# Dense TensorE products in the waits of the first units, and two bonus products on VectorE

## The chip, the cores and the metric

The kernel runs on one core of a Trainium2 chip. The metric is the device time of one execution in microseconds (us); three runs of the kernel before are given, and one execution was profiled. [...]

## The reference, cut to what matters

An RWKV-like attention with a state per head, then a soft mixture of experts, then a feed-forward layer with a squared ReLU. The change touches the attention alone:

```python
B, H, S, D = r.shape                      # 4, 8, 768, 48
for t in range(S):
    kt, vt, rt = (k[:, :, t], v[:, :, t], r[:, :, t])
    cur = np.einsum('bhd,bhe->bhde', u[None] * kt, vt)
    y[:, :, t] = np.einsum('bhd,bhde->bhe', rt, state + cur)
    state = w[None, :, :, None] * state + np.einsum('bhd,bhe->bhde', kt, vt)
```

The part with `u` is the bonus: token t sees its own key and value with the weight sum over d of r * u * k.

## The kernel before, in words

The attention is cut into 16 units (NU): a batch and a pair of heads each, n = 0 to 15. A unit has six chunks of 128 tokens (NC), taken in two groups g of three (GC). Each unit has r, k transposed (`tr`, loaded by L92 in two halves) and k, r, v with tokens on the partitions (`krv`, loaded by L96 in two halves) in one of four buffers (NB), so the loads of unit n + 4 are issued when unit n has let go of its buffer.

The steps of a unit are small functions, and the order of the instructions on each engine is the order in which they are called (the schedule is written out by hand; each engine runs its own queue in order):

- `decay(n, m)`, L232: VectorE multiplies the transposed r (m = 0) or k (m = 1) by a table of powers of w, which lies in PSUM (`tab`).
- `bonus(n)`, L237 and L238: GpSimd multiplies r by u, then by k, both in place. Each product is 128x576.
- `weigh(n)`, L242: VectorE sums that over d into `dg`, the diagonal's values.
- `keys(n)`, L248: GpSimd (VectorE for unit 0) multiplies k by powers of w (`pkn`).
- `diag(n, g)`, L254: GpSimd spreads `dg` onto the diagonal of `AT` by an affine select. AT has three buffers.
- `A(n, g)`, L264: TensorE makes the scores of three chunks and two heads, in two PSUM banks; `strict(n, g)`, L270: VectorE copies the part above the diagonal into `AT` and so frees the two banks.
- `KV(n)`, L278: TensorE makes the sums over a chunk of k times v; `scan(n)`, L283: VectorE scans them over the chunks, and ScalarE copies the result to `SB` (L285).
- `Y(n, g)`, L301 and L307: TensorE multiplies by the state and by AT; ScalarE copies out (L313).
- `X(n, g)`, L320, and `L(n)`, L335: TensorE turns the outputs and makes the logits of the experts, one unit later.
- `keep_clock(k)`, L225: k fp32 products of the identity with itself, 128x128 by 128x256, into a bank of the tag "tr" that nobody reads. The trace shows each as two instructions.

Ahead of the loop stand the tables: the powers of w on VectorE (L193 to L208), their transposes on TensorE (L424), the copy to `pkn` (L425), and the first steps of unit 0 (L417 to L438). In the loop, iteration n calls A(n, 1); keys, weigh, diag(., 0) and decay(., 1) of unit n + 1; strict(n, 1); X(n - 1, 0); Y(n, 0); KV(n + 1) and diag(n + 1, 1); L(n - 1); A(n + 1, 0), scan and strict(n + 1, 0); X(n - 1, 1); Y(n, 1); bonus(n + 2) and decay(n + 2, 0); and then the loads of unit n + 4 and mostly one load of an expert's weights (1536 KB).

After the attention come the experts (L540 to L582) and the feed-forward layer (L725 to L817), whose weights are loaded as buffers come free.

Of the kernel before, what the change touches and what calls it, by code (L numbers as in the profile page):

```python
# [24 lines left out]
ALU = mybir.AluOpType  # L25
# [4 lines left out]
def rwkv_softmoe_ffn(ctx: ExitStack, tc: tile.TileContext, tr, krv, wt, u, phi, w1, w2, w_in, w_out, out):  # L30
    nc = tc.nc
    NU, _, _, S = tr.shape
    D = phi.shape[0] // (2 * wt.shape[1])
    NROW, NHALF = 12 * (S // 128) * D // 2, krv.shape[-1] // 2
    NP = wt.shape[1]
    H = 2 * NP
    B = NU // NP
    NC = S // 128
# [21 lines left out]
    def ps(tag):  # L60
        cnt[0] += 1
        return psum.tile([128, 512], F32, name=f"ps_{tag}{cnt[0]}", tag=tag, bufs=BANKS[tag])

    def wk(shape, tag, bufs, dt=F32, pool=None):
        cnt[0] += 1
        return (pool or work).tile(shape, dt, name=f"{tag}_{cnt[0]}", tag=tag, bufs=bufs)
# [14 lines left out]
    def t_view(n):  # L81

        return units[n % NB][:112, :2 * S].rearrange("p (m c t) -> p m c t", m=2, c=NC)

    def n_view(n):

        return units[n % NB][:, 2 * S:].rearrange("p (m c h d) -> p m c h d", m=3, c=NC, h=2)
# [13 lines left out]
    U = att.tile([128, NP, 2, D], F32, name="U")  # L101
# [95 lines left out]
    for i in range(6):  # L197
        n = 1 << i
# [21 lines left out]
    def keep_clock(n):  # L220

        if n:
            p = ps("tr")
        for _ in range(n):
            nc.tensor.matmul(p[:, :256], ident, ident.unsqueeze(1).to_broadcast([128, 2, 128]), start=True, stop=True)  # L225


    def decay(n, m):

        x = t_view(n)[:, m]  # L230
        t = tab[:, n % NP] if m else tab[:, n % NP, ::-1]
        nc.vector.tensor_tensor(x, x, t.unsqueeze(1).to_broadcast([112, NC, 128]), ALU.mult)  # L232

    def bonus(n):

        kv_, rv = n_view(n)[:, 0], n_view(n)[:, 1]
        nc.gpsimd.tensor_tensor(rv, rv, U[:, n % NP].unsqueeze(1).to_broadcast([128, NC, 2, D]), ALU.mult)  # L237
        nc.gpsimd.tensor_tensor(rv, rv, kv_, ALU.mult)  # L238

    def weigh(n):  # L240
        dg = wk([128, NC, 2], "dg", 2)
        nc.vector.reduce_sum(dg, n_view(n)[:, 1], axis=AX.X)  # L242
        st[n, "dg"] = dg
# [6 lines left out]
    def diag(n, g):  # L250
        at = wk([128, GC, 2, 128], "AT", 3, pool=att)
        st[n, "AT", g] = at
        dg = st[n, "dg"][:, GC * g:GC * (g + 1)]
        nc.gpsimd.affine_select(out=at.rearrange("p c h t -> p (c h) t"),  # L254
                                in_=dg.rearrange("p c h -> p (c h)").unsqueeze(2).to_broadcast([128, 2 * GC, 128]),
                                pattern=[[0, 2 * GC], [1, 128]], compare_op=ALU.is_equal, fill=0.0, base=0, channel_multiplier=-1)

    def A(n, g):
        tv = t_view(n)
        p = [ps("A")[:, :GC * 128].rearrange("p (c t) -> p c t", c=GC) for _ in range(2)]  # L260
        for i in range(GC):
            for h in range(2):
                rows = slice(64 * h, 64 * h + D)
                nc.tensor.matmul(p[h][:, i], tv[rows, 1, GC * g + i], tv[rows, 0, GC * g + i], start=True, stop=True)  # L264
        st[n, "A", g] = p

    def strict(n, g):
        at, p = st[n, "AT", g], st.pop((n, "A", g))
        for h in range(2):
            nc.vector.copy_predicated(at[:, :, h], mask.unsqueeze(1).to_broadcast([128, GC, 128]), p[h])  # L270

    def KV(n):

        kv_, vv = n_view(n)[:, 0], n_view(n)[:, 2]
        pv = kvp[:, :D * NC].rearrange("p (d c) -> p d c", c=NC)
        for c in range(NC - 1):
            for h in range(2):
                nc.tensor.matmul(pv[64 * h:64 * h + D, :, c + 1], kv_[:, c, h], vv[:, c, h], start=True, stop=True)  # L278
# [8 lines left out]
    def Y(n, g):  # L287
        vv, tv = n_view(n)[:, 2], t_view(n)
        at, s = st.pop((n, "AT", g)), SB[n % 2]

        p = [y.rearrange("p (c t) -> p c t", t=128) for y in yp]
        chunks = range(GC * g, GC * (g + 1))
        at_of = lambda c, j: p[c % 2][64 * j:64 * j + D, (c - chunks[c % 2 != chunks[0] % 2]) // 2]
        opened = set()
        for c in chunks:
            for h in range(2 if c > 0 else 0):
                rows, j = slice(64 * h, 64 * h + D), (h + c) % 2  # L300
                nc.tensor.matmul(at_of(c, j), s[rows, c], tv[rows, 0, c],  # L301
                                 start=(c % 2, j) not in opened, stop=True, skip_group_check=True)
                opened.add((c % 2, j))
        for c in chunks:
            for j in range(2):
                h = (j + c) % 2
                nc.tensor.matmul(at_of(c, j), vv[:, c, h], at[:, c - GC * g, h],  # L307
                                 start=False, stop=True, skip_group_check=True)
        if g == 0:
            st[n, "xT"] = wk([112, NC, 128], "xT", 2, pool=att)  # L310
        for k in range(2):
            c0 = chunks[k]
            nc.scalar.copy(st[n, "xT"][:, c0:GC * (g + 1):2], p[c0 % 2][:112, :len(chunks[k::2])])  # L313
# [34 lines left out]
    def soft_exp(b):  # L348

        eT = wk([96, 2, 256], "eT", 1)  # L350
        st["eT", b] = eT
        nc.scalar.activation(eT[:, 0], st["lg", b][:96, :256], AF.Exp, bias=st["nm", b])
        nc.scalar.copy(eT[:, 1], st["lg", b][:96, :256])
        if 0 < b < B - 1:
            new = st["new", b]
            fa, fb = wk([96, 1], "fa", 2), wk([96, 1], "fb", 2)
            nc.scalar.activation(fa, nmx[:, 0:1], AF.Exp, bias=new, scale=-1.0)
            nc.scalar.activation(fb, st["nm", b], AF.Exp, bias=new, scale=-1.0)
            nc.scalar.copy(nmx[:, 0:1], new)
            st["f", b] = fa, fb  # L360
# [53 lines left out]
    nc.gpsimd.affine_select(out=maskf, in_=maskf, pattern=[[1, 128]], compare_op=ALU.is_gt, fill=0.0,  # L414
                            base=0, channel_multiplier=-1)
    nc.gpsimd.tensor_copy(mask, maskf)
    bonus(0)  # L417
    decay(0, 1)
    decay(0, 0)
    keep_clock(6)  # L420

    pp = ps("lg")
    for a in range(NP):
        nc.tensor.transpose(pp[:, a * 128:a * 128 + 112], tabs[:, a], ident[:112, :112])  # L424
    nc.scalar.copy(pkn, pp.rearrange("p (a b d) -> p a b d", a=NP, b=2)[:, :, :, :D])  # L425
    A(0, 0)
    weigh(0)
    diag(0, 0)
    keys(0, nc.vector)
    nc.scalar.copy(carry[:, :, :, 1:], pw[:, 0, :NP].unsqueeze(2).unsqueeze(3).to_broadcast([112, NP, D, NC - 1]))  # L430
    KV(0)
    strict(0, 0)
    scan(0)
    diag(0, 1)
    for i in range(2):
        nc.gpsimd.memset(xn[i][:, :, DM:DM + 1], 1.0)
    bonus(1)
    decay(1, 0)  # L438
    nload = 0
    for n in range(NU):  # L440
        nxt = n + 1 < NU
        if n == 2:

            sel = const.tile([128, 4, NS], F32, name="sel")
            nc.vector.reduce_sum(sel, ident.rearrange("p (q s) -> p s q", q=4).unsqueeze(1).to_broadcast([128, 4, NS, 4]), axis=AX.X)
            rm = const.tile([128, E], F32, name="rm")
            nc.vector.reduce_sum(rm, ident.rearrange("p (q e j) -> p e q j", q=4, e=E), axis=AX.XY)
            ones = const.tile([1, 4], F32, name="ones")
            nc.gpsimd.memset(ones, 1.0)

        b, j = divmod(n, NP)
        b -= 1
        A(n, 1)
        if nxt:
            keys(n + 1)
            weigh(n + 1)
            diag(n + 1, 0)
            decay(n + 1, 1)
        strict(n, 1)
        if n > 0:  # L460
            X(n - 1, 0)
        if b >= 0 and j == 1:
            soft_exp(b)
        Y(n, 0)
        if b >= 0 and j == 2:
            soft_sum(b)
            slots_exp(b)
        if nxt:
            KV(n + 1)
            diag(n + 1, 1)  # L470
        if n > 0:
            L(n - 1)

        if nxt:
            A(n + 1, 0)
            scan(n + 1)
            strict(n + 1, 0)
        if n > 0:
            X(n - 1, 1)
        if not nxt:  # L480
            L(n, (0,))
            X(n, 0)
        Y(n, 1)
        if b >= 0 and j == 1:
            soft_turn(b)
        if n + 2 < NU:
            bonus(n + 2)
            decay(n + 2, 0)
        if b >= 0 and j == 0:
            soft_max(b)  # L490
        if b >= 0 and j == 2:
            slots_norm(b)
        if n + NB < NU:
            load_t(n + NB)
            load_n(n + NB)
            if n not in (1, 4, 7):
                load_weight(nload)
                nload += 1
        elif n == NU - 2:
            load_win(0)  # L500
        else:
            load_weight(nload)
            nload += 1
# [382 lines left out]
```

## Time and profile before

| what | value |
|---|---|
| median of three runs | 400.87 us (400.12 to 401.17) |
| the profiled execution's own time | 400.18 us |
| its span, first to last instruction | 398.5 us |
| mean granted clock | 0.973 |
| TensorE busy | 381.7 us, 96% of the span |
| VectorE busy | 280.2 us, 70% |
| ScalarE busy | 211.7 us, 53% |
| GpSimd busy | 114.8 us, 29% |
| share of TensorE in the chain that ended last | 80% |

Shares of busy time are means over stages that differ: GpSimd works almost only in the first third of the span, and there it is busy nearly all the time. A busy TensorE is not TensorE at its peak, since matmuls are pipelined and their ends are modelled; so starts of instructions say more than their lengths.

### The profile page before, as it was taken

How to read it: one execution, taken by the hardware profiler on the slowest of the kernel's cores; microseconds unless marked ns; L12 is line 12 of the kernel's file. 1: busy time of each engine (PE TensorE's matmuls, PEld its weight loads, DVE VectorE, ACT ScalarE, POOL GpSimd, SP SyncE). 2: the span in 40 equal slices, each digit the busy share in tenths (PEclk: the TensorE clock that was granted, in tenths of full speed). 3: DMA queues.
4: the chain of work that ended last, by engine and by line, in shares of the span. 5: the costliest groups of instructions: out<-in, count | busy, mean ns of one | idle time of the engine just before them, and what ended most of it. 6: DMA issues, size and time to landing. Idle time of an engine off the chain costs nothing.

```text
span 398.5 us, 8194 instructions
## 1 busy us (share of the span) xinstructions
PE 381.7 (96%) x3219; PEld 294.2 (74%) x3219; DVE 280.2 (70%) x495; ACT 211.7 (53%) x465; POOL 114.8 (29%) x110
## 2 busy tenths in 40 slices
PE   5799999999999999789999999999999999999995
PEld 3677777767766564668787888888888888888884
DVE  5769897879974564799998567666566676566563
ACT  2224453453444451678888876555554564554552
POOL 3869997986870001122323120000000000000000
PEclk8559999999999999999999999999999999999999
DMA  7999999999995899913333202100000040000004
GB/s 245 344 320 343 389 407 403 404 404 406 405 383 188 307 410 405 375 47 102 85 100 87 63 0 104 56 0 2 0 0 2 0 159 2 0 0 2 0 0 158
DMA packets 25989, 70.81 MB, mean 178 GB/s; under 512 B 3680, under 2 KB 6112, under 8 KB 25952
## 3 DMA queue, kind: packets, MB, share of 16 engines
q1 hardware_dynamic: 25808, 70.10, 47.2%
q10 hardware_dynamic: 144, 0.20, 0.5%
q8 instruction: 25, 0.41, 0.4%
q14 instruction: 12, 0.10, 0.1%
HBM read 64.78 MB, written 4.72 MB: 174 GB/s over the span
## 4 chain that ended last, share of the span: by engine, by line
PE 80%; DMA 9%; DVE 6%; POOL 2%; issue 1%; ACT 1%; SPq 0%; POOLq 0%; ACTq 0%; DVEq 0%
PE ps_Y L817 16%; PE ps_A L817 16%; PE ps_kv L817 8%; PE ps_lg L817 8%; PE ps_A L264 7%; DMA wo<-in_w_out_dram 7%; PE ps_Y L307 5%; PE ps_Y L301 3%; PE ps_tr L320 3%; PE ps_tr L725 3%; PE ps_tab L725 3%; PE ps_lg L335 2%; DMA slot<-in_krv_dram 2%; PE ps_kv L278 2%; PE ps_tr L378 1%
## 5 line engine op out<-in xcount | busy, mean ns | idle before, releaser
L817 PE MATMUL ps_Y<-slot,slot 128*128 128x512 f32 x288 | 111.7, 395 | 0.0
L750 DVE TENSOR_TENSOR slot<-gg,slot 128x512 fp32r<-128x512 f32 (+1 forms) x97 | 66.5, 685 | 49.2 <-ACT slot L747 48.3
L817 PE MATMUL ps_A<-slot,slot 128*128 128x512 f32 x288 | 88.9, 393 | 0.6 <-DVE slot L682 0.6
L747 ACT CAST slot<-gg 128x512 fp32r<-128x512 f32 (+1 forms) x97 | 59.8, 618 | 50.5 <-DVE gg L744 49.9
L817 PEld LDWEIGHTS ps_A<-slot,slot 128*128 128x128 f32 x288 | 54.0, 188 | 13.2 <-DVE slot L682 1.0
L817 PEld LDWEIGHTS ps_Y<-slot,slot 128*128 128x128 f32 x288 | 54.1, 188 | 12.6 <-issue 0.6
L744 DVE TENSOR_TENSOR gg<-hr 128x512 f32<-128x512 f32 (+1 forms) x71 | 49.0, 691 | 14.3 <-ACT hr L737 14.2
L817 PE MATMUL ps_kv<-slot,slot 128*128 128x512 f32 x144 | 55.7, 394 | 0.0
L817 PE MATMUL ps_lg<-slot,slot 128*128 128x512 f32 x144 | 55.4, 391 | 0.0
L623 POOL TENSOR_TENSOR slot<-wf,slot 128x384 fp32r<-128x384 f32 x16 | 19.1, 1196 | 97.5 <-ACT slot L618 97.5
L270 DVE COPY_PREDICATED AT<-mask,ps_A 128x384 f32<-128x384 int32 x64 | 33.8, 583 | 9.2 <-PE ps_A L264 8.4
L264 PE MATMUL ps_A<-slot 48*128 48x128 f32 x384 | 36.2, 310 | 2.9 <-DVE slot L232 1.8
L264 PEld LDWEIGHTS ps_A<-slot 48*128 48x128 f32 x384 | 28.7, 204 | 10.3 <-DVE AT L270 3.6
L737 ACT ACTIVATE hr<-ps_tab 128x512 f32<-128x512 f32 x48 | 28.7, 599 | 12.9 <-PE ps_tab L725 12.9
L737 ACT ACTIVATE hr<-ps_tr 128x512 f32<-128x512 f32 (+1 forms) x49 | 28.8, 590 | 12.4 <-PE ps_tr L725 12.4
L313 ACT COPY xT<-ps_Y 112x256 f32<-112x256 f32 x64 | 17.4, 324 | 28.0 <-PE ps_Y L307 27.8
L254 POOL TENSOR_SCALAR_AFFINE_SELECT AT<-dg 128x768 f32<-128x768 f32 x32 | 28.0, 886 | 13.2 <-PE ps_Y L307 8.4
L817 PEld LDWEIGHTS ps_kv<-slot,slot 128*128 128x128 f32 x144 | 27.1, 188 | 6.2
L817 PEld LDWEIGHTS ps_lg<-slot,slot 128*128 128x128 f32 x144 | 27.0, 188 | 5.9
L232 DVE TENSOR_TENSOR slot<-slot,ps_tab 112x768 f32<-112x768 f32 x32 | 30.1, 941 | 0.6 <-DMA slot<-in_tr_dram 0.6
L307 PE MATMUL ps_Y<-AT,slot 128*48 128x128 f32 x384 | 29.6, 293 | 0.0
L307 PEld LDWEIGHTS ps_Y<-AT,slot 128*48 128x48 f32 x384 | 20.8, 129 | 6.5 <-issue 5.9
(168 smaller groups left out, 502.3 us busy)
## 6 DMA issues: line engine op xcount, KB each, us to landing
slot<-in_w_dram SPq DMA_DIRECT2D x14, 1536.0 KB, 11.1
slot<-in_tr_dram SPq DMA_DIRECT2D x32, 384.0 KB, 7.5
slot<-in_krv_dram SPq DMA_DIRECT2D x16, 448.0 KB, 7.3
slot<-in_krv_dram SPq DMA_DIRECT2D x16, 416.0 KB, 7.8
slot<-in_w_in_dram SPq DMA_DIRECT2D x4, 1536.0 KB, 19.1
wo<-in_w_out_dram SPq DMA_DIRECT2D x16, 384.0 KB, 3.3
out_dram<-os SPq DMA_DIRECT2D x15, 256.0 KB, 2.2
post<-in_w_dram SPq DMA_DIRECT2D x2, 1536.0 KB, 9.2
```

What stands on the lines that cost most here:

```text
L232: nc.vector.tensor_tensor(x, x, t.unsqueeze(1).to_broadcast([112, NC, 128]), ALU.mult)
L254: nc.gpsimd.affine_select(out=at.rearrange("p c h t -> p (c h) t"), in_=dg.rearrange("p c h -> p (c h)").unsqueeze(2).to_broadcast([128, 2 ...
L264: nc.tensor.matmul(p[h][:, i], tv[rows, 1, GC * g + i], tv[rows, 0, GC * g + i], start=True, stop=True)
L270: nc.vector.copy_predicated(at[:, :, h], mask.unsqueeze(1).to_broadcast([128, GC, 128]), p[h])
L307: nc.tensor.matmul(at_of(c, j), vv[:, c, h], at[:, c - GC * g, h], start=False, stop=True, skip_group_check=True)
L623: nc.gpsimd.tensor_tensor(wout_half(wls, f, WL), st.pop(("wf", f)), hi, ALU.subtract)
L725: nc.tensor.matmul(p, gst[:, 128 * f:128 * (f + 1)], cTall[:, 512 * g:512 * (g + 1)], start=True, stop=True)
L737: nc.scalar.activation(fs[i, "hr"][:, c], fs[i, "p"][:, c], AF.Relu)
L744: nc.vector.tensor_mul(gg, hr, hr)
L747: nc.scalar.copy(part(i, "gh")[:, c], fs[i, "gg"][:, c])
L750: nc.vector.tensor_tensor(part(i, "gl")[:, c], fs[i, "gg"][:, c], fs[i, "gh"].bitcast(F32)[:, c], ALU.subtract)
L817: nc.tensor.matmul(o, (hi, lo, hi)[k][:, 128 * j:128 * (j + 1)], (gh, gh, gl)[k], start=(f == 0 and k == 0), stop=(f == NF - 1 and k == 2))
```

## The change

The first product of the bonus can be put on another engine, and for units 0 and 1 that is VectorE; the second stays on GpSimd. The call of bonus(1) and that of diag(0, 1) move ahead of strict(0, 0) and scan(0). keep_clock is called with 13 in place of 6 ahead of the transposes of the table, and is called anew: 3 behind these transposes, 1 behind A(0, 0), 1 ahead of Y(0, 0) and 3 behind it (in the loop, for n = 0 alone).

```diff
-    def bonus(n):
+    def bonus(n, eng=nc.gpsimd):
 
         kv_, rv = n_view(n)[:, 0], n_view(n)[:, 1]
-        nc.gpsimd.tensor_tensor(rv, rv, U[:, n % NP].unsqueeze(1).to_broadcast([128, NC, 2, D]), ALU.mult)
+        eng.tensor_tensor(rv, rv, U[:, n % NP].unsqueeze(1).to_broadcast([128, NC, 2, D]), ALU.mult)
         nc.gpsimd.tensor_tensor(rv, rv, kv_, ALU.mult)
...
-    bonus(0)
+    bonus(0, nc.vector)
     decay(0, 1)
     decay(0, 0)
-    keep_clock(6)
+    keep_clock(13)
 
     pp = ps("lg")
     for a in range(NP):
         nc.tensor.transpose(pp[:, a * 128:a * 128 + 112], tabs[:, a], ident[:112, :112])
     nc.scalar.copy(pkn, pp.rearrange("p (a b d) -> p a b d", a=NP, b=2)[:, :, :, :D])
+    keep_clock(3)
     A(0, 0)
+    keep_clock(1)
     weigh(0)
     diag(0, 0)
     keys(0, nc.vector)
...
     KV(0)
+    diag(0, 1)
+    bonus(1, nc.vector)
     strict(0, 0)
     scan(0)
-    diag(0, 1)
     for i in range(2):
         nc.gpsimd.memset(xn[i][:, :, DM:DM + 1], 1.0)
-    bonus(1)
     decay(1, 0)
...
+        if n == 0:
+            keep_clock(1)
         Y(n, 0)
+        if n == 0:
+            keep_clock(3)
```

## Rows read from the trace of the kernel before

**Rows 1.** The page, slices: TensorE's granted clock in tenths, 40 equal slices.
```profile
PEclk8559999999999999999999999999999999999999
```

**Rows 2.** Busy by stretch: us, PE, PEld, DVE, ACT, POOL busy, PEclk, DMA share, GB/s.
```profile
28.00:29.00 1.00, 1.00 (x29) 0.94 (x28) 0.00 (x0) 0.40 (x2) 0.42 (x1) 0.81 0.83 312
...
173.20:176.60 3.40, 2.25 (x29) 1.39 (x28) 3.37 (x6) 2.94 (x6) 1.57 (x1) 1.00 0.38 118
```

**Rows 3.** Timeline of TensorE, start: start us, length us, instruction, [idle before <-releaser].
```profile
1.43 2.93 PE L225 MATMUL ps_tr<-ident 128*128 128x256 f32 x6 [1.43 <-POOL ident masks.py:199]
...
4.76 1.03 PE L225 MATMUL ps_tr<-ident 128*128 128x256 f32 x4
...
8.57 1.01 PE L424 MATMUL ps_lg<-ident,xT 112*128 112x112 f32 x4 [2.79 <-ACT xT L210]
```

**Rows 4.** The chain that ended last, 18 to 36 us: start us, us, what.
```profile
18.86 1.04 PE ps_kv L278 x20
...
27.05 1.45 PE ps_Y L307 x12
28.50 0.45 PE ps_kv L278 x20
...
29.52 0.87 PE ps_A L264 x12
30.39 0.44 PE ps_tr L320 x3
30.83 0.57 PE ps_Y L301 x12
31.40 0.79 PE ps_Y L307 x12
...
33.50 0.37 PE ps_Y L301 x8
...
34.66 0.45 PE ps_kv L278 x20
```

**Rows 5.** Timeline of all engines, 8.5 to 18 us.
```profile
8.52 1.41 POOL L237 TENSOR_TENSOR slot<-slot,U 128x576 f32<-128x576 f32 x1 [5.64 <-DMA slot<-in_krv_dram]
...
9.42 1.86 DVE L232 TENSOR_TENSOR slot<-slot,ps_tab 112x768 f32<-112x768 f32 x2 [0.58 <-DMA slot<-in_tr_dram]
...
10.00 1.41 POOL L238 TENSOR_TENSOR slot<-slot 128x576 f32<-128x576 f32 x1
...
12.11 0.75 DVE L248 TENSOR_TENSOR slot<-slot,pkn 128x576 f32<-128x576 f32 x1
12.27 2.13 POOL L254 TENSOR_SCALAR_AFFINE_SELECT AT<-dg 128x768 f32<-128x768 f32 x2 [0.86 <-DVE dg L242]
...
13.62 1.05 DVE L270 COPY_PREDICATED AT<-mask,ps_A 128x384 f32<-128x384 int32 x2 [0.76 <-POOL AT L254]
...
14.26 2.11 PE L264 MATMUL ps_A<-slot 48*128 48x128 f32 x12 [0.30 <-DVE AT L270]
...
15.34 0.63 ACT L285 COPY SB<-sc 112x240 f32<-112x240 f32 x1 [4.35 <-DVE sc L283]
...
17.40 1.40 POOL L248 TENSOR_TENSOR slot<-slot,pkn 128x576 f32<-128x576 f32 x1
```

**Rows 6.** Instructions of L225 and of L254: ns min/median/max, first and last start us.
```profile
L225 PE MATMUL ps_tr<-ident x14: 379/520/793, 1.4 to 129.5; 128*128 128x256 f32 x14
...
L254 POOL TENSOR_SCALAR_AFFINE_SELECT AT<-dg x32: 859/866/1315, 12.3 to 116.9; 128x768 f32<-128x768 f32 x32
```

**Rows 7.** Timeline: keys(2) and bonus(8) on GpSimd, KV(8) on TensorE.
```profile
23.39 1.41 POOL L248 TENSOR_TENSOR slot<-slot,pkn 128x576 f32<-128x576 f32 x1
...
61.55 1.42 POOL L237 TENSOR_TENSOR slot<-slot,U 128x576 f32<-128x576 f32 x1 [0.16 <-DMA slot<-in_krv_dram]
...
67.78 0.62 PE L278 MATMUL ps_kv<-slot 128*48 128x48 f32 x20
```

**Rows 8.** Busy by stretch, 25 to 40 us (columns as in rows 2).
```profile
25.00:40.00 15.00, 15.00 (x223) 11.50 (x219) 10.96 (x18) 5.29 (x18) 11.21 (x11) 0.89 0.88 326
```

## The prediction, made before the change was timed

> **What bounds the kernel now.** I read the slices of the page first: the granted clock is low in the first three slices and full from the fourth on (9 is 90% or more) [rows 1]. A slice is 9.96 us: the first is in the 0.8s, so the fall comes some 6.0 to 7.9 us into it, nearer the end by the idle time below; the next two are in the 0.5s, and a finer stretch averages 0.81 from 28 to 29 us [rows 2], so the rise comes near 28.4 us. [...] What TensorE did before the fall stands in its timeline: six keep_clock calls (twelve products, since each fp32 matmul is two) start at 1.43 us, the last four of them 0.216 us apart; then the engine idles 2.79 us until the transposes of the decay table at 8.57 us [rows 3], and in that idle time the clock falls. Then I read the chain that ended last. From 18.86 us it is TensorE alone, piece after piece with no gap: KV(1), A(1,0), Y(0,1) in two pieces, A(1,1), X(0,0), Y(1,0) in two pieces, eight pieces up to 28.50 us, all at half clock (the first and the last of the eight stand in [rows 4]). Before 18.86 us the chain lies on GpSimd: bonus(1) in two products, then keys(1), and KV(1) waits for them [rows 4, 5]. So the start is slow for two reasons: TensorE at half clock, and before that three GpSimd products of 1.41 us in a row.
>
> **The extra products at the start.** 13 calls make 26 products instead of 12. The first six take 2.93 us with the pipeline's tail of the last, so under 0.49 us each, and I take 0.45; the last four of before start 0.216 us apart ((1.03 - 0.38) / 3, 0.379 us being the shortest product from start to end) [rows 3, 6]. The twelfth starts at 5.40, the 26th at 5.40 + 14 x 0.216 = 8.43, and its stream ends near 8.65 us. The transposes wait for ScalarE's table until 8.57 anyway, so they start 0.1 us late, which nothing on the path sees: their result is first read by keys(0) at 12.11 us [rows 5]. The next three calls are 6 x 0.216 = 1.3 us, to about 10.4; A(0,0) cannot start before the two decays are done at 11.3 us [rows 3, 5]. Cover: the wait for the decays. The single call behind A(0,0) takes 0.43 us and ends before KV(0)'s keys at 12.87 us. All three cost nothing; at half clock they would cost 0 to 2 us (below).
>
> **The bonus of unit 0 on VectorE.** The GpSimd product of 1.41 us at 8.52 us [rows 5] becomes a VectorE one. That price is not in the trace for this line; the nearest row is keys(0), the same shape on VectorE, 0.75 us [rows 5], and I take that. VectorE is free at 8.84 us (it idled 0.58 us before the decays at 9.42 [rows 5]), so it runs 8.84 to 9.59, and GpSimd's second product ends at 11.06 instead of 11.41. But the two decays stand behind it on VectorE: they end at 11.45 instead of 11.28, and weigh(0) behind them starts at 11.45, where it waited for GpSimd until 11.41 before. A saving of 0.35 us on GpSimd is eaten by the queue of VectorE: 0.
>
> **The bonus of unit 1 on VectorE, and the reorder.** VectorE gets a second 0.75 us between keys(0) and strict(0,0), to 13.6 us; strict started at 13.62, so by itself it is hidden. It also waits there for unit 1's load, with strict and A(0,1) queued behind. But GpSimd's first select ran beside keys(0) and took 1315 ns where the median is 866 [rows 6]: two-operand VectorE work stretched it by 0.45 us. With a second such product right behind, I let the select end near 14.2 instead of 13.58 us (bounds: 0 if nothing is stretched, 0.75 if all of the product is). So strict(0,0), the scan behind it and ScalarE's SB copy [rows 5] each come 0.6 us later: SB at 16.55 instead of 15.97. A(0,1) starts at 14.85, is done by 16.1 at full clock (it ended at 16.37), one keep_clock call (0.43) lies in the wait for SB, Y(0,0) runs 16.6 to 17.8 (0.37 + 0.79 [rows 4]). GpSimd: second select to 15.05, second product of bonus(1) to 16.5, two memsets, keys(1) to 18.1 instead of 18.81 us: 0.7 us sooner, the 1.4 us of the removed product less the stretch. Three keep_clock calls behind Y(0,0) take 1.3 us, to 19.15. **They are longer than their hole**: KV(1) could start at 18.1 and starts at 19.15 instead, 0.3 us later than 18.86.
>
> **The clock behind it.** If the clock holds, the eight pieces take 0.45 + 0.87 + 0.57 + 0.79 + 0.87 + 0.44 + 0.37 + 0.79 = 5.15 us (full-clock rows of the same pieces [rows 4]) instead of 28.50 - 18.86 = 9.64: 4.5 us. KV(2) can start at 24.3 instead of 28.50, 4.2 us sooner. GpSimd must have keys(2) by then: it ended at 24.80 [rows 7], now 0.7 sooner, 24.1. A unit is 6.16 us of TensorE (KV(2) at 28.50 to KV(3) at 34.66) and 3 x 1.49 (the step from product to product) + 2 x 0.87 = 6.2 us of GpSimd [rows 4 to 6]; for KV(3) that is 30.3 on GpSimd against 30.45 on TensorE. It just fits; I take 0.2 us off for these thin margins. Gain: **4.0 us**, bounds 3.4 (stretch of the whole product, one more late start) to 4.8 (no stretch).
>
> [...]
>
> **Does it last to the end?** In the attention TensorE is the path from here on, and each unit's loads are issued by what TensorE has finished, so they move along. Loads have little room: bonus(8) waited 0.16 us for its load, but KV(8) at 67.78 us came 1.8 us after 61.55 + 3 x 1.49 [rows 7]. DMA had idle time to give: its share averaged 0.88 from 25 to 40 us [rows 8], so 15 x 0.12 = 1.8 us. The last weights and the loads behind the attention are issued when TensorE frees their buffers, so that wait moves too.
>
> **The rivals.** (a) The clock falls again for a while, or rises late: partial gain. For: TensorE still idles about 1.1 us before A(0,0) and 1.3 us before A(0,1). Against: at full clock, the stretch from 173.2 us has 2.25 us busy of 3.40 and keeps 1.00 [rows 2]. A fall at 14.7 that is over at 18 gives about 2.9 us; if all 26 first products run at 0.45 us, they end at 13.1 us, pkn and keys(0) come 2 us late, and 2 us remain. So a gain of 1 to 3, about 398.8. [...] (b) **Slower**: the clock falls before A(0,1) and rises no sooner than before. Then the added calls are paid at half clock: A(0,1) 14.85 + 2.11 = 16.96 [rows 5], one call 0.9, Y(0,0) 1.16 x 9.64 / 5.15 = 2.2, three calls 2.7: KV(1) at 22.75, 3.9 us late. If the rise still comes at 28.4, 59% of the eight pieces are done by then and the rest takes 2.1 us, to 30.5: 2.0 us lost; if it needs the same work first, 3.9. So 402.9 to 404.8. The point is a rise at about 24.0 us: with a later one the change loses. (c) The loads become the bound: TensorE's lead ends at unit 8, and the gain is 1.8 us (no earlier DMA) to 3.6 (all 1.8 us of idle used): about 398. (d) No effect: the extra products keep the clock only until the first gap, and their cost is hidden: 400.9.
>
> **The numbers.** The profiled execution took 400.18 us (span 398.5), 0.69 under the median of the three runs. The sum gives 396.2 on it and 396.9 on the median; as part of the runs' spread of 1.05 us may be the clock rising at different times, which the change would take away, I say 396.6. Own range of the likeliest case: 395.2 to 397.5. Chances: forecast 0.67, (a) 0.13, (b) 0.08, (c) 0.07, (d) 0.05. The range of 8 in 10 takes in (a) and (c) down to a gain of some 1.5 us: 395.2 to 399.4. A measurement tells 0.3%, 1.2 us, from no change; so faster 0.83, same 0.09, slower 0.08.
>
> **What would show it.** Right: granted clock 1.00 in every stretch from about 5 us on; 26 products to about 8.7 us; strict(0,0) near 14.2 and KV(1) near 19.1 us with keep_clock products right before it; KV(2) near 24.3; FFN unchanged but 4 us earlier. Wrong: a clock of 0.50 after 14 us (a, b); GpSimd's first products of later units waiting for krv loads (c); a select that isn't stretched (gain up to 4.8); keep_clock calls that take 0.45 us per product.

## The result and the profile after

The changed kernel takes 397.04 us (median of 4 runs, 396.35 to 397.56) against 401.02 us before (4 runs, 400.12 to 402.04): a ratio of 0.9899, 95% interval 0.9870 to 0.9928, 4.0 us faster. The profiled execution took 397.56 us, its span is 395.8 us. The granted clock is TensorE's, as a share of full speed; the traces before and after have two levels of it, 0.50 and 1.00. Executions of one kernel differ by 0.8 us (the five of c3 below) to 6.4 us (eleven of the kernel before, beside e5), and the mean granted clock can differ with them (e2 below: 0.984 to 0.987 in the eight executions from 395.3 to 397.1 us, 0.973 to 0.976 in the four from 399.7 us on), so it stands beside an execution's time where that matters. The ratios leave out executions more than 1.5% above the fastest of their kernel.

First the slices of the page of the kernel after, the granted clock in tenths, to be laid beside [rows 1]:

```profile
PEclk9999999999999899999999999999999999999999
```

The half-clock stretch at the start is gone (in both profiles the very first products start 0.43 us apart instead of 0.216, see the last section). A single slice, the 14th (from 128.6 us), is under 0.9, and it is new: before, the clock was full there.

The start on VectorE and GpSimd, timeline of the kernel after (start us, length us, instruction, idle before it), beside [rows 5]:

```profile
8.40 0.76 DVE L237 TENSOR_TENSOR slot<-slot,U 128x576 f32<-128x576 f32 x1
9.33 1.86 DVE L232 TENSOR_TENSOR slot<-slot,ps_tab 112x768 f32<-112x768 f32 x2 [0.17 <-DMA slot<-in_tr_dram]
11.11 0.75 DVE L242 TENSOR_REDUCE dg<-slot 128x12 f32<-128x576 f32 x1
11.77 0.75 DVE L248 TENSOR_TENSOR slot<-slot,pkn 128x576 f32<-128x576 f32 x1
12.51 1.34 DVE L237 TENSOR_TENSOR slot<-slot,U 128x576 f32<-128x576 f32 x1
13.78 1.04 DVE L270 COPY_PREDICATED AT<-mask,ps_A 128x384 f32<-128x384 int32 x2
```

```profile
11.93 2.65 POOL L254 TENSOR_SCALAR_AFFINE_SELECT AT<-dg 128x768 f32<-128x768 f32 x2 [1.27 <-DVE dg L242]
14.55 1.40 POOL L238 TENSOR_TENSOR slot<-slot 128x576 f32<-128x576 f32 x1
...
16.03 1.42 POOL L248 TENSOR_TENSOR slot<-slot,pkn 128x576 f32<-128x576 f32 x1
```

The same product on VectorE takes 0.76 us for unit 0 and 1.34 us for unit 1; the two selects take 2.65 us where they took 2.13; keys(1) ends at 17.45 us instead of 18.81. TensorE then has the path, as the chain that ended last shows (beside [rows 4]):

```profile
16.43 0.37 PE ps_Y L301 x8
16.80 0.79 PE ps_Y L307 x12
17.59 1.49 PE ps_tr L225 x6
19.08 0.58 PE ps_kv L278 x20
19.67 0.87 PE ps_A L264 x12
...
23.57 0.79 PE ps_Y L307 x12
24.36 0.45 PE ps_kv L278 x20
```

The three calls behind Y(0,0) (L225) stand on the path with 1.49 us, KV(1) follows at 19.08, and the eight pieces take 24.36 - 19.08 = 5.28 us instead of 9.64. By the timeline, which shows the first matmul of a group, KV(1) starts at 19.01 and KV(2) at 24.19 instead of 28.29 us, 4.1 us sooner. The lead lasts through the attention: KV(15), in the timeline of the kernel after and then of the kernel before, again 4.09 us apart:

```profile
114.13 0.38 PE L278 MATMUL ps_kv<-slot 128*48 128x48 f32 x7
```

```profile
118.22 0.38 PE L278 MATMUL ps_kv<-slot 128*48 128x48 f32 x8
```

Behind it a part is given back in this execution. Busy time by stretch of the kernel after (columns as in [rows 2]), and the first TensorE work in the slow stretch:

```profile
124.00:127.00 3.00, 2.08 (x15) 1.02 (x13) 1.00 (x4) 1.69 (x6) 0.00 (x0) 1.00 0.48 150
128.00:131.00 3.00, 3.00 (x15) 0.85 (x10) 0.48 (x2) 0.44 (x2) 0.00 (x0) 0.50 0.59 243
```

```profile
127.81 2.79 PE L378 MATMUL ps_tr<-xn,en 128*32 128x385 f32 x12 [0.21 <-ACT en L371]
```

At the end of the attention TensorE has little to do, and the clock then runs at 0.50 from 127.7 to 131.1 us. Little to do is not enough to bring that about: the kernel before is as thin in the same steps (2.46 us busy of 3.40, below, and 2.48 of 3.40 in the kernel after from 124.2 us on), and its clock held:

```profile
128.30:131.70 3.40, 2.46 (x17) 1.42 (x16) 1.00 (x4) 1.66 (x7) 0.00 (x0) 1.00 0.70 214
```

The twelve products of the last soft_sum take 2.79 us in this execution; in another profiled execution of the same kernel (c1_change below), where the clock held too, they take 1.50:

```profile
128.29 1.50 PE L378 MATMUL ps_tr<-xn,en 128*32 128x385 f32 x12 [0.21 <-ACT en L371]
```

The first load of w_out, issued by what follows, comes at 137.45 us against 139.99: 2.5 of the 4.1 us are left. In c1_change it comes at 136.38, with KV(15) at 114.62: 3.6 us of lead at both places.

### The profile page after: what moved, and what is told of

It reads as the page before. It is cut to its first block, busy times and chain, and to the rows that moved or that the text cites. A ratio compares the mean times of both kernels' runs of the same rounds, so it can differ in the third digit from the quotient of the medians.

```text
span 395.8 us, 8254 instructions
## 1 busy us (share of the span) xinstructions
PE 382.8 (97%) x3249; PEld 294.3 (74%) x3249; DVE 282.0 (71%) x497; ACT 211.2 (53%) x465; POOL 111.9 (28%) x108
## 4 chain that ended last, share of the span: by engine, by line
PE 81%; DMA 9%; DVE 7%; issue 1%; ACT 1%; SPq 0%; DVEq 0%; ACTq 0%
PE ps_Y L823 16%; PE ps_A L823 16%; PE ps_kv L823 8%; PE ps_lg L823 8%; PE ps_A L264 7%; DMA wo<-in_w_out_dram 7%; PE ps_Y L307 5%; PE ps_Y L301 3%; PE ps_tr L320 3%; PE ps_tr L731 3%; PE ps_tab L731 3%; PE ps_lg L335 2%; PE ps_tr L378 2%; DMA slot<-in_tr_dram 2%; PE ps_kv L278 2%; DVE slot L232 2%
## 5 line engine op out<-in xcount | busy, mean ns | idle before, releaser
L264 PE MATMUL ps_A<-slot 48*128 48x128 f32 x384 | 33.2, 291 | 2.5 <-DVE AT L270 1.9
L264 PEld LDWEIGHTS ps_A<-slot 48*128 48x128 f32 x384 | 25.9, 187 | 9.8 <-DVE AT L270 4.9
L254 POOL TENSOR_SCALAR_AFFINE_SELECT AT<-dg 128x768 f32<-128x768 f32 x32 | 28.5, 901 | 10.9 <-PE ps_Y L307 5.7
L307 PE MATMUL ps_Y<-AT,slot 128*48 128x128 f32 x384 | 27.6, 279 | 0.0
L238 POOL TENSOR_TENSOR slot<-slot 128x576 f32<-128x576 f32 x16 | 22.6, 1413 | 7.5 <-DVE slot L237 6.4
```

## The experiments

The first four kernels, and then c1 to c4, ran on one chip; the kernel before took 401.17 us beside the first four (17 runs) and 401.27 beside c1 to c4 (11 runs). e5, e6, e7 and e9 ran on another chip, where it took 404.09 us (11 runs, 399.72 to 406.11). Ratios are to the kernel before, run beside the changed one.

**The clock alone (e1).** All added calls, bonus and order as before.

```diff
-    bonus(0, nc.vector)
+    bonus(0)
...
-    diag(0, 1)
-    bonus(1, nc.vector)
     strict(0, 0)
     scan(0)
+    diag(0, 1)
...
+    bonus(1)
```

> All keep_clock calls of the change, both bonus products and the order as before. Theory (the gain is the clock's): granted clock 1.00 from about 5 us on; keys(1) ends at 18.8 us as before, so KV(1) starts near 19.0 as it does with the change; but GpSimd has keys(2) only at 24.8 in place of about 23.5, so KV(2) starts near 24.9 against 24.19: 3.3 to 3.6 us faster than before, about 397.6. Rival (the products taken off GpSimd bring a good part of it): the gain is 2.5 us or less, 398.5 or more.

Measured: 396.46 us, ratio 0.9890 (0.9869 to 0.9912). In the profiled execution the granted clock is 1.00 in every stretch from 5 to 25 us, and the first products become quick near 6.6 us; KV(1) at 18.91, KV(2) at 24.90 us, as the theory had it, behind keys(2) on GpSimd:

```profile
23.44 1.41 POOL L248 TENSOR_TENSOR slot<-slot,pkn 128x576 f32<-128x576 f32 x1
```

```profile
24.90 0.66 PE L278 MATMUL ps_kv<-slot 128*48 128x48 f32 x20
```

The profiled execution, 396.38 us, is 3.8 us under the one before. So the calls alone bring nearly all of the gain, in five of six executions (396.1 to 397.4 us). The sixth took 402.34 us at a mean granted clock of 0.987; it was not profiled and is not in the ratio.

**The moved products alone (e2).** No added call, 6 at the start. The moved products and the new order stay together; no run parts them.

```diff
-    keep_clock(13)
+    keep_clock(6)
...
-    keep_clock(3)
     A(0, 0)
-    keep_clock(1)
...
-        if n == 0:
-            keep_clock(1)
         Y(n, 0)
-        if n == 0:
-            keep_clock(3)
```

> Both bonus products on VectorE and the new order, keep_clock as before (6 calls at the start, none added). Theory: the clock is at 0.50 from about 8 to 28 us as before; KV(1) waits for TensorE at half clock instead of GpSimd and starts near 18.5 in place of 18.86: 0 to 0.5 us faster, about 400.7. Rival (GpSimd sets the start): KV(1) near 17.5 and 1.3 us faster, about 399.7.

Both were wrong. 12 runs fall into two groups: eight from 395.3 to 397.1 us, with a mean granted clock of 0.984 to 0.987, and four from 399.7 to 401.0 with 0.973 to 0.976; the median is 395.96. The profiled execution is of the first group. Busy time by stretch:

```profile
10.00:15.00 5.00, 3.33 (x36) 2.94 (x38) 5.00 (x8) 0.27 (x1) 3.86 (x4) 0.56 1.04 354
15.00:20.00 5.00, 5.00 (x57) 4.31 (x58) 4.29 (x7) 1.17 (x3) 4.61 (x7) 0.50 0.99 362
20.00:25.00 5.00, 5.00 (x87) 3.96 (x85) 4.19 (x8) 1.82 (x6) 4.64 (x5) 0.91 1.00 374
```

The clock falls after the start as before, but is back near 21 us instead of 28.4. From 15 to 20 us TensorE is busy all 5.00 us. The kernel before had 4.56 there, but it too was busy all 5.00 us from 20 to 25 us, and stayed at 0.50 until 28.4:

```profile
15.00:20.00 5.00, 4.56 (x53) 3.45 (x52) 3.73 (x6) 1.17 (x3) 4.84 (x5) 0.50 0.96 338
20.00:25.00 5.00, 5.00 (x44) 4.04 (x46) 4.17 (x6) 1.17 (x3) 4.84 (x5) 0.50 0.95 346
```

KV(1) started at 18.25 us, near the theory's 18.5, but at KV(2), 24.53, this kernel is only 0.3 us behind the full change. So without any added call the clock comes back some 7 us sooner, in most executions: none of the 28 executions of the kernel before that stand beside e1 to e4 and c1 to c4 had a mean granted clock over 0.977. That the closed wait before KV(1) is what brings it back is argued, not shown.

**Without the three calls behind Y(0,0) (e3).**

```diff
         Y(n, 0)
-        if n == 0:
-            keep_clock(3)
```

> The change without the three keep_clock calls behind Y(0,0). Theory (they are longer than their hole): the clock holds without them, KV(1) starts near 17.6 in place of 19.01, then GpSimd is the limit with keys(2) near 23.4, and KV(2) starts near 23.5 in place of 24.19: 0.4 to 0.7 us faster than the change, about 396.4. Rival (these calls hold the clock): a stretch of 0.50 begins between 18 and 22 us, and it is 1 us or more slower than the change.

Measured: 396.80 us, ratio 0.9895 (0.9875 to 0.9914). KV(1) at 17.41 and KV(2) at 23.40 us with the clock full, as the theory had it: the calls are 1.6 us too long for their hole, and keys(2) on GpSimd then sets KV(2):

```profile
17.41 0.66 PE L278 MATMUL ps_kv<-slot 128*48 128x48 f32 x20
23.40 0.66 PE L278 MATMUL ps_kv<-slot 128*48 128x48 f32 x20
```

```profile
21.94 1.41 POOL L248 TENSOR_TENSOR slot<-slot,pkn 128x576 f32<-128x576 f32 x1
```

But the lead over the change shrinks from 0.8 us at KV(2) to 0.5 at KV(15) (113.66 us): bonus(8) waits 0.69 us for its load instead of 0.20, and the step from KV(8) to KV(9) takes 6.90 us instead of 6.56. In the time e3 can't be told apart from the change.

**Only the later calls (e4).**

```diff
-    keep_clock(13)
+    keep_clock(6)
...
-    keep_clock(3)
     A(0, 0)
```

> The change with 6 calls in place of 13 at the start and without the three behind the transposes; the five later calls and the bonus products stay. Theory: the clock falls near 8 us as before, and the denser work from 11 us on brings it back between 18 and 22 us, some 7 us sooner than before: about half of the gain, 398.5 to 399.5. Rival (b of the prediction: it rises no sooner than before): the five calls are paid at half clock and it is slower than before, 402 or more.

Measured: 398.56 us, ratio 0.9944 (0.9921 to 0.9966): as the theory had it. The clock falls near 9.4 us and is back near 19.7, but the late calls are partly paid at half clock, the single one with 1.22 us for its two products:

```profile
16.48 1.22 PE L225 MATMUL ps_tr<-ident 128*128 128x256 f32 x2
```

KV(1) comes at 21.18 us, 2.9 us later than with e2, and KV(2) at 26.37, 1.8 later. In these two profiled executions the late calls at half clock are worse than none; between the times the intervals overlap a little (e2: 0.9900, 0.9868 to 0.9932).

**Calls at the end of the attention (e5, e6).** e5 adds two single calls to the change, into the bank of the tag "tab"; e6 also leaves out the three behind Y(0,0).

```diff
-    def keep_clock(n):
+    def keep_clock(n, tag="tr"):
...
-            p = ps("tr")
+            p = ps(tag)
...
     X(NU - 1, 1)
+    keep_clock(1, "tab")
     soft_turn(B - 1, slice(0, 1))
...
+    keep_clock(1, "tab")
     soft_sum(B - 1)
```

> The change with two more single keep_clock calls at the end of the attention, one in the wait for xn behind the last X, one ahead of the last soft_sum. Theory (the half-clock stretch from 127.7 us in the profile of the change, which TensorE's thin work there brings on, costs 1.0 to 1.3 us wherever an execution has it): all executions hold 1.00 there, mean granted clock 0.996 or more in each, and the median comes 0.5 us under the change's 397.04, about 396.5. Rival (the stretch costs nothing, since the loads behind the attention set the time): the median stays within 0.2 us of 397.04 or rises by the two calls, 0.4 us.

> Both: without the three calls behind Y(0,0), and with the two single calls at the end of the attention. Theory: the lead of the run without the three calls (KV(15) at 113.7 us against 114.1) and no half-clock stretch: about 396.0, the fastest so far. Rival (without the three calls the clock is less safe): some executions with a mean granted clock under 0.99 and a median of 397 or more.

Measured on the other chip: e5 398.55 us, ratio 0.9894 (0.9844 to 0.9945); e6 398.26 us, 0.9875 (0.9829 to 0.9922). The expected microseconds can't be compared, since the start is later there: the load of w lands 5.7 us after its issue in all four profiles, instead of 3.1 to 3.5 in the other ten (L99's time to landing), VectorE's table starts that much later, and strict(0,0) starts at 16.2 us. In e5's profiled execution, the slowest of its six, the clock falls between 18 and 23 us (mean 0.66), behind a wait of 1.18 us for strict(0,0); at the attention's end it held in both. What the end calls are worth alone stays open.

**bonus(0) back on GpSimd (e7).**

```diff
-    bonus(0, nc.vector)
+    bonus(0)
```

> The change with the first product of bonus(0) back on GpSimd. Theory (what GpSimd saves there VectorE's queue takes back): weigh(0) starts at most 0.3 us later, KV(1) and KV(2) start within 0.2 us of the change: the same time within 0.3 us, about 397. Rival (the 0.35 us saved on GpSimd is on the path): 0.4 to 0.6 us slower, 397.5 or more.

Measured on that chip: 400.82 us, ratio 0.9953 (0.9900 to 1.0005), 2.3 us over e5, which also has the two calls at the attention's end. That is the rival's size and more; the traces show an effect that neither theory nor rival had. VectorE's table products (L199) in e7, then in e5:

```profile
8.97 1.23 DVE L199 TENSOR_TENSOR P<-P,pw 112x128 f32<-112x128 f32 x1
...
10.52 1.30 DVE L199 TENSOR_TENSOR P<-P,pw 112x256 f32<-112x256 f32 x1
```

```profile
8.96 0.29 DVE L199 TENSOR_TENSOR P<-P,pw 112x128 f32<-112x128 f32 x1
...
9.57 0.43 DVE L199 TENSOR_TENSOR P<-P,pw 112x256 f32<-112x256 f32 x1
```

and GpSimd in e7:

```profile
8.66 1.40 POOL L237 TENSOR_TENSOR slot<-slot,U 128x576 f32<-128x576 f32 x1 [5.78 <-DMA slot<-in_krv_dram]
10.13 1.41 POOL L238 TENSOR_TENSOR slot<-slot 128x576 f32<-128x576 f32 x1
```

Each table product that starts beside one of GpSimd's ends 0.1 to 0.3 us behind it (10.20 against 10.06 us, 11.82 against 11.54). The decays start at 12.92 instead of 11.63 us, and strict(0,0) at 17.49 instead of 16.20. Where w lands by 4.3 us, the last table product is over (7.77 us in the kernel before) ahead of GpSimd's product, which begins at 8.5 us [rows 5], and took 0.43 us. But the two profiled executions don't show the 2.3 us: in both the clock falls for a while, in e7 before A(0,0) (mean 0.57 from 13 to 17 us), in e5 before Y(0,0) (0.66 from 18 to 23), and e7's KV(1) starts at 22.75, 0.2 us ahead of e5's. So the stretch of the table products is shown, and what it costs in the end stays open.

**Only the calls at the start (e9).**

```diff
     A(0, 0)
-    keep_clock(1)
...
-        if n == 0:
-            keep_clock(1)
         Y(n, 0)
-        if n == 0:
-            keep_clock(3)
```

> The change with only the first 13 calls and the 3 behind the transposes; the 1, 1 and 3 later ones are gone. Theory (with the bonus off GpSimd the waits from 11 us on are short enough for the clock): 1.00 from about 5 us on, KV(1) near 17.4, KV(2) near 23.4 us, as without the three calls: about 396.6. Rival (the single calls hold the clock in the two waits of some 1 us): the clock falls between 11 and 19 us, and the time is 397.5 or more.

Measured on that chip: 401.57 us, ratio 0.9964 (0.9904 to 1.0023): the rival. Two of six executions hold the clock (0.996; 398.6 and 398.8 us), the others have 0.972 to 0.981. In the profiled one, 404.12 us, it falls twice: at 11.2 us, behind a wait of 2.1 us for the table, to be back at 14.6, and again at 18.0, behind the wait of 1.06 us for strict(0,0), to be back only at 31.6:

```profile
11.00:15.00 4.00, 4.00 (x22) 2.99 (x21) 4.00 (x7) 1.37 (x2) 2.20 (x2) 0.57 1.02 329
15.00:18.00 3.00, 1.94 (x37) 1.53 (x34) 2.24 (x5) 0.04 (x1) 3.00 (x3) 1.00 1.02 377
18.00:25.00 7.00, 6.79 (x78) 5.43 (x77) 5.76 (x9) 1.75 (x4) 6.70 (x9) 0.50 0.81 305
25.00:31.00 6.00, 6.00 (x67) 4.66 (x66) 2.78 (x6) 1.54 (x6) 2.79 (x4) 0.50 0.96 339
31.00:35.00 4.00, 4.00 (x61) 2.99 (x57) 2.93 (x5) 1.58 (x5) 3.87 (x4) 0.92 0.87 324
```

This is rival (b) of the prediction in kind: a fall ahead of the units' work, and no gain left in this execution. e6, on the same chip, keeps the two single calls and lacks the three behind Y(0,0), and none of its six executions, nor of e5's, has a mean under 0.993. In e9, without them, 2 of 6 are that high. So where the start is late, the two single calls may help to hold the clock; e5 and e6 also have the two calls at the attention's end, and e7 on the same chip, with the single calls and without those at the end, has 0.982 to 0.989 in three of six.

**The change, e6, e2 and one more, side by side (c1 to c4)** on the first chip. c2 and c3 are the kernels of e6 and e2; c4 undoes one edit of the change:

```diff
-    bonus(1, nc.vector)
+    bonus(1)
```

> The change itself once more, beside the three below on one chip. Theory (start of the table's chain sets the rest: where the load of w lands near 6.5 us in place of 4, all steps of unit 0 come 2.3 us later and TensorE's waits are that much longer): 3.5 to 5 us faster than before on any chip, with a half-clock stretch in some executions. Rival (the gain hangs on one chip's early loads): under 2 us where w lands late.

> The change without the three calls behind Y(0,0) and with the two at the attention's end, beside the change on one chip. Theory: 0.4 to 1.2 us faster than the change in the same call (0.3 to 0.6 from KV(1) to KV(15), and no half-clock stretch at the attention's end). Rival: the same within 0.3 us, since the loads behind the attention take it back.

> Both bonus products on VectorE and the new order, no added keep_clock call, beside the change on one chip. Theory (the clock comes back by itself when TensorE's work is dense enough, which differs from execution to execution): two groups of times, one within 0.5 us of the change or under it with a mean granted clock near 0.984, one about 1 us under before with 0.973 to 0.976; where w lands late, more of the second. Rival (the moved products bring the gain, whatever the clock): one group, within 1 us of the change.

> The change with the first product of bonus(1) back on GpSimd, behind the second select. Theory: keys(1) ends 1.4 us later, near 18.8 us where w lands early, and keys(2) near 24.9, so KV(2) starts 0.7 us later than with the change: 0.5 to 0.8 us slower than the change. Rival (the longer waits let the clock fall): 1.5 us or more slower, with half-clock stretches before 25 us.

| kernel | median us | ratio to before, 95% interval | KV(2) us | KV(15) us |
|---|---|---|---|---|
| c1, the change | 396.23 | 0.9875 (0.9847 to 0.9904) | 24.33 | 114.62 |
| c2, e6 | 395.90 | 0.9863 (0.9836 to 0.9891) | 24.15 | 114.08 |
| c3, moved products alone | 395.79 | 0.9865 (0.9834 to 0.9896) | 24.49 | 114.40 |
| c4, bonus(1) on GpSimd | 396.46 | 0.9884 (0.9853 to 0.9915) | 24.56 | 115.48 |

The intervals overlap: nothing here is shown faster than the change. c1 repeats the gain (5.0 us), and w landed early (4.2 us), so the change itself wasn't tried where it lands late; e5 is the nearest to it there. c2's median is 0.3 us under c1's, less than these runs can tell. Its profiled execution had a stretch at half clock between 15 and 20 us (mean 0.66); it begins at 15.9 us, ahead of the place of the three calls that c2 leaves out, and up to there c2 is the same program as c1, where the clock held. So it says nothing about those calls, only that the start of the change can lose the clock for a while too. All five runs of c3 are of e2's first group (0.984 to 0.987), which neither its theory nor its rival excludes. c4's keys(2) ends at 24.5 us, 0.9 later than c1's, but KV(2) comes only 0.2 later. By KV(15) it is 0.9 behind, since bonus(8) waits 1.97 us for its load (0.74 in c1), and its profiled execution took 0.8 us more. Between the medians it is 0.2 us, not told apart.

## Why the prediction was right, point by point

- **What bounds it, and the eight pieces**: right. Forecast 5.15 us at full clock, measured 5.28; KV(1) forecast at 19.15, started at 19.01; KV(2) 24.3 and 24.19; gain at the end of the attention 4.0 and 4.09. The slow first products of the kernel before, 0.43 us apart until some 4.5 us, are another thing than the stretch at half clock that the change takes away: that begins with a fall at 7.9 us, after the products had become quick.
- **The calls at the start cost nothing**: right. The 26th product starts at 8.57 us and the transposes at 8.79, 0.2 us later than before; A(0,0) still waits 0.60 us for the decays. In c1, where some 13 of the 26 products are slow instead of 8, the transposes start at 9.87 and A(0,0) at 11.65, 0.3 us behind the decays; strict(0,0), which waits for the select, starts at 13.91 all the same.
- **bonus(0) is worth 0**: nearly right for loads of w that land early. weigh(0) starts at 11.24 us in c1 and at 11.44 in the kernel before, where w landed at the same time within 0.1 us: 0.2 us, and strict(0,0) shows none of it, as bonus(1) takes it back (next point). It fails where w lands late: there two table products take 1.23 and 1.30 us beside GpSimd's instead of 0.29 and 0.43, and strict(0,0) comes 1.3 us later (17.49 in e7, 16.20 in e5), at a price in time that is open. I had read only what the product saves on GpSimd and costs in VectorE's queue, not what GpSimd's two products do to VectorE.
- **"I let the select end near 14.2"**: the step that was mis-sized. I had the select stretched by both VectorE products. It took 1312 ns and ended at 13.24, no longer than beside keys(0) alone before (1315 [rows 6]); bonus(1)'s product ended 0.61 us behind it, after 1.34 us instead of 0.75, and the second select behind that product, after 1376 ns where the median is 863 (L254's durations). strict(0,0) started at 13.78, only 0.16 us late, not 0.6, and keys(1) ended at 17.45, not 18.1. The 0.65 us did not show, since the three calls behind Y(0,0) covered it; that KV(1) came within 0.15 us of its forecast is luck in that part. On the other chip it went as the prediction feared: beside both products the select took 1982 ns in e5.
- **"They are longer than their hole"**: right, and by more: 1.5 us (19.01 against 17.45). e3 shows what lies behind it: KV(2) 0.8 us sooner, then GpSimd is the limit.
- **Lasting to the end**: right in the attention of this execution (bonus(8) waited 0.20 us for its load). In c1 it waited 0.74 us, and the step from KV(8) to KV(9) took 6.96 us instead of 6.56: 0.4 us taken back there, behind the load. Not foreseen: the fall at the attention's end, which took 1.5 us of the profiled execution's lead and is why it took 397.56 and not the 396.2 that the sum gave on it. Nor did the change take away the runs' spread, for which the prediction went 0.3 us under its sum: it was 1.05 us in the three runs before, and is 1.2 in the four of the change and 2.4 in the six of c1.
- **The rivals**: (a) and (b) are real. In the change the clock held through the start in both profiled executions, and e9 shows the fall once waits grow and the later calls are missing. (c) came in small, the 0.4 us above; (d) did not come.
- **Where the gain comes from**: the sum was right, its reading was too narrow. I put the 4.5 us on the added calls and 0.7 us on GpSimd. Shown by e1, e2 and c3: each part alone brings nearly all of it, and together they bring no more. The traces show why the sum is no larger than its parts: KV(2) comes at 24.2 to 24.9 us in all three, each time behind another limit. With the calls alone GpSimd sets it (keys(2) ends at 24.85), with the moved products alone the half clock until 20.9 us does, and with both the three calls behind Y(0,0). That the clock is back some 7 us sooner with the moved products and no added call (e2) was not among the prediction's rivals. What the calls add may be safety: e2 and c3 lost the gain in 4 of 17 executions, the change in none of its 10 (394.9 to 397.6 us, mean granted clocks of 0.993 and up), which is too few to be sure, and e1, with all the calls, had its one execution of 402.34 us. Where w lands late there is more to it: 4 of 6 executions of e9 have a mean granted clock under 0.982, and none of the 12 of e5 and e6 is under 0.993; but three of e7's six, with all the calls, have 0.982 to 0.989.

## What to carry to other kernels

Here closing TensorE's waits (e2, ratio 0.9900) and filling them with idle products (e1, 0.9890) were substitutes: the change, with both, has 0.9899. Try each alone before adding both, and look at every execution's granted clock, since one profile shows one case. A filler belongs where the clock is still full and is no longer than its hole; paid at half clock (1.22 us for a call in e4 instead of 0.70), or ahead of work that is ready (e3: 0.8 us at KV(2)), it costs. Before moving a product between GpSimd and VectorE, read what runs beside it on the other (e7: a table product of 0.29 us took 1.23).

## What the runs showed of the hardware

Some instructions of VectorE and GpSimd that ran beside each other were stretched, and ended in turn. On VectorE bonus(1)'s product, beside the selects, took 1344 ns, where bonus(0)'s, with GpSimd idle, took 759; the select that ended behind it took 1376 ns, where the median of the 32 is 863; a table product beside a GpSimd product took 1.23 us in e7, and 0.29 in e5 with GpSimd idle. In the kernel after, keys(0) ends at 12.52 us, the first select at 13.24, bonus(1)'s product at 13.85 and the second select at 14.58: 0.72, 0.61 and 0.73 us apart, each a little less than the instruction takes unstretched. The one that starts first does not always end first. In e5 the select starts at 14.18 us, and bonus(1)'s product on VectorE, which starts at 14.69, ends ahead of it, unstretched; the select ends at 16.16, after 1982 ns:

```profile
14.69 0.75 DVE L237 TENSOR_TENSOR slot<-slot,U 128x576 f32<-128x576 f32 x1
```

TensorE's first products become quick at different times in executions that begin alike. They start 0.43 us apart and then 0.216, a ratio of two as between the clock's levels: the change of pace comes near 4.5 us in the profile before, near 6.6 in e1's, and in e2's not within the twelve products. The same twelve, in the profile before (first) and in e2's:

```profile
1.43 4.36 PE L225 MATMUL ps_tr<-ident 128*128 128x256 f32 x12 [1.43 <-POOL ident masks.py:199]
```

```profile
1.42 5.49 PE L225 MATMUL ps_tr<-ident 128*128 128x256 f32 x12 [1.42 <-POOL ident masks.py:199]
```

The granted clock of the profile does not show this: it reads 1.00 from the start of the span, and the mean granted clocks above count these first products as full. In the kernel before, four products in one microsecond, 0.43 us apart:

```profile
3.00:4.00 1.00, 1.00 (x4) 0.82 (x3) 0.00 (x0) 0.00 (x0) 0.00 (x0) 1.00 1.00 128
```

And a small load differed: w landed 5.7 us after its issue in the four profiles of the second chip, 3.1 to 3.5 in the other ten; strict(0,0) starts at 16.20 us in e5, at 13.78 in the kernel after. Whether all executions on the second chip had it is not shown; the kernel before took 399.7 to 406.1 us there.
